# Retention scores in 64x64 quadrants, ordered ahead of the state product, with k transposed unscaled

## The chip, the cores and the metric

The kernel runs on one core of one Trainium2 chip. The metric is device time in microseconds (us) of one execution, as the median of several runs. Engines are named as in the profile: PE (TensorE's matmuls), PEld (its weight loads), DVE (VectorE), ACT (ScalarE), POOL (GpSimd) and SP (SyncE, which issues most transfers).

## What is computed

Retention attention (scores with a decay of gamma to the distance, no softmax), then a mixture of experts with a noisy gate that picks two of eight, then a second dense layer pair. The change is in the attention alone:

```python
def _attn_ref(q, k, v):                      # (4, 8, 576, 64)
    scale = 1.0 / np.sqrt(D_)
    scores = scale * np.matmul(q, k.transpose(0, 1, 3, 2))
    gamma = 1.0 - 2.0 ** (-5.0 - np.arange(H, dtype=np.float32))
    rel = pos[:, None] - pos[None, :]
    Dmat = np.where(rel >= 0, gamma[:, None, None] ** rel[None, :, :], 0.0)
    return np.matmul(scores * Dmat, v)

def reference(**kwargs):
    attn_out = _attn_ref(**attn_kwargs)
    x = attn_out.transpose(0, 2, 1, 3).reshape(B * S, H * D)     # 2304 x 512
    x = _moe_ref(x=x, **moe_kwargs)          # gate, two experts of eight, w1, relu, w2
    return _moe2_ref(x=x, **moe2_kwargs)     # x @ w_in, gated, @ w_out
```

## The kernel before

The 2304 tokens are 18 tiles `t` of 128. A sequence has 576 tokens, four and a half tiles, so a pattern of nine tiles repeats (`m = t % 9`): tiles with m = 0 begin a sequence and have no state yet, tiles with m = 4 hold the end of one sequence and the start of the next, and tiles with m = 8 add nothing to the state. The eight heads lie in pairs: `a` is the pair, and a head of a pair takes 64 of the 128 rows.

A tile takes these steps. `load` brings k, q and v on SP's queue, three tiles ahead. `ks` and `qs` scale k and q by powers of gamma on DVE. `tr` transposes k (four 128x128 transposes on PE) and ACT evicts the result as `kT`. q arrives in a layout that needs no transposition. `qk` computes the scores of 128 keys by 128 queries for each head into two PSUM banks (`sc0`, `sc1`; tags `ga` and `gb`, one buffer each), and DVE multiplies each bank by a mask of zeros and ones into `pt`. `av` multiplies the state of the tiles before (`sbd`, 64x64 for each head) by q into `px` (two banks, of which one has the tag `tp` with a single buffer). `av2` adds masked scores times v to `px`, and ACT evicts `px` with a scale into `xT`. `kv` adds k transposed times v to the state in PSUM (`pS`), which ACT evicts to `sbd` for the next tile. `xt` transposes the output back to rows of tokens, which ACT evicts to `xrow`. For every three tiles `gsum` and `logit` compute the gate's logits.

The gate's routing is a generator, `route`, one for each group of three tiles. Its parts are divided by `yield`, and `rstep` runs the next part, so the places of `rstep` in the loop fix where the route's instructions stand on each engine. On DVE the parts are: copying the logits, four operations on `rw`, four that end in `nl`, MAX to `rd`, and the one-hot part `ixf`, `rm`, `ra`. The rank matmuls (L374 to L377) multiply `ra` by a triangle and by ones on PE, and a last DVE part turns the ranks into slots. `send` scatters a token tile's rows to the experts' regions in DRAM from POOL. `wstep` splits expert weights into two parts for the next stage, on ACT and DVE, in the later tiles.

The order of work is written out by hand in the loop of `attention`; each engine works through its instructions in that order. In an iteration `t` it is: `xt` of t - 1, `tr` of t + 2, `av`, `av2`, `kv`, scaling for t + 3, `qk` and the masks of t + 1, `gsum` on every third. Five `rstep` lie between. Ahead of the loop `busy` runs matmuls on zeros (`BZ`: 7, then 2), and `table` makes a table of decays for q from a small transfer `grow`.

## Time and profile before

| what | us |
|---|---|
| median of 3 runs | 947.82 |
| lowest and highest run | 944.35, 948.03 |
| profiled execution, its own time | 936.64 |
| its span in the trace | 934.5 |
| PE busy | 921.8 (99%) |
| DVE busy | 606.8 (65%) |
| ACT busy | 466.5 (50%) |
| POOL busy | 235.9 (25%) |

The attention ends where the experts' first matmul (L737) begins, at 95.07 us of the span; the rest of the span belongs to the two layers behind it. In a timeline, the first number is the start in us from the span's start, the second the time until the last of the row's instructions ended, and a bracket at the end tells how long the engine was idle ahead and what released it. Matmuls overlap, so the length of a step on PE is best read from its start to the start of the next.

### The profile page before, as it was taken

Reading aid. Unit: us, or ns where it says so; the run is one execution under the profiler, and the core shown is the slowest. Engines: PE = TensorE matmul, PEld = TensorE weight load, DVE = VectorE, ACT = ScalarE, POOL = GpSimd, SP = SyncE. Lnnn points to the kernel's source line nnn. Section 1 sums busy time; section 2 is a strip of 40 time slices with the busy share of each in tenths; the row PEclk is TensorE's granted clock in tenths of the full one; section 3 lists DMA queues with packets and bytes.
Section 4 is the critical chain, followed back from the end, with each engine's and each line's share of the span. In section 5 each row is a group of like instructions: output and inputs, shape, how many; then the busy total and the mean of one; then the engine's idle time right before and its main releaser. Section 6 shows DMA issues by size and latency. Waiting matters only on the chain.

```text
span 934.5 us, 17789 instructions
## 1 busy us (share of the span) xinstructions
PE 921.8 (99%) x6314; PEld 818.2 (88%) x6314; DVE 606.8 (65%) x1327; ACT 466.5 (50%) x1025; POOL 235.9 (25%) x324
## 2 busy tenths in 40 slices
PE   9999999999999999999999999999999999999996
PEld 6887888988988889888888899999889998999985
DVE  5787747878879797787847446545745554564442
ACT  4666435455564645545544445544554464455432
POOL 1345531324233242432400221042004113300000
PEclk9999999999999999999999999999999999999999
DMA  9964877859879688896636787877578676846541
GB/s 339 386 243 147 304 243 232 238 187 280 259 241 282 227 256 271 248 267 218 224 111 214 265 298 252 307 247 240 188 262 270 205 258 227 271 166 228 167 150 49
DMA packets 123742, 221.22 MB, mean 237 GB/s; under 512 B 13037, under 2 KB 60915, under 8 KB 123643
## 3 DMA queue, kind: packets, MB, share of 16 engines
q1 hardware_dynamic: 113819, 190.47, 61.9%
q0 software_dynamic: 9392, 28.73, 9.1%
q8 instruction: 52, 0.85, 0.4%
q10 hardware_dynamic: 432, 0.79, 0.2%
q14 instruction: 47, 0.39, 0.1%
HBM read 163.97 MB, written 55.97 MB: 235 GB/s over the span
## 4 chain that ended last, share of the span: by engine, by line
PE 86%; DVE 7%; DMA 3%; issue 1%; ACT 1%; POOL 1%; SPq 0%; DVEq 0%; ACTq 0%; POOLq 0%
PE p L754 39%; PE ga L737 12%; PE gb L737 9%; PE mga L1168 7%; PE p L1168 5%; PE mgb L1168 2%; PE mtp L1168 2%; PE sc L225 2%; DVE b L591 1%; PE px L249 1%; PE p L293 1%; DVE cvt L635 1%; PE p L209 1%; DMA xe<-s,free 1%; DVE h L796 1%
## 5 line engine op out<-in xcount | busy, mean ns | idle before, releaser
L754 PE MATMUL p<-b,h 128*120 128x512 f32 (+1 forms) x1056 | 260.9, 395 | 0.0
L754 PEld LDWEIGHTS p<-b,h 128*120 128x120 f32 (+1 forms) x1056 | 189.2, 185 | 41.4 <-DVE h L796 0.4
L754 PE MATMUL p<-b,b 128*128 128x512 f32 x768 | 180.0, 390 | 0.0
L754 PEld LDWEIGHTS p<-b,b 128*128 128x128 f32 x768 | 142.3, 188 | 28.2
L737 PE MATMUL ga<-x,b 128*128 128x360 f32 (+1 forms) x768 | 134.4, 324 | 2.9 <-DVE h L796 2.9
L737 PEld LDWEIGHTS ga<-x,b 128*128 128x128 f32 x768 | 124.6, 188 | 12.1 <-DVE h L796 7.7
L640 POOL TENSOR_TENSOR cvl<-cvl,cvs 128x256 f32<-128x256 f32 x64 | 50.3, 785 | 229.9 <-ACT cva L621 163.0
L591 DVE TENSOR_TENSOR b<-b,b 128x512 fp32r<-128x512 f32 x128 | 89.6, 734 | 13.2 <-ACT b L590 12.9
L737 PE MATMUL gb<-b,b 128*128 128x256 f32 x672 | 89.7, 283 | 0.0
L737 PEld LDWEIGHTS gb<-b,b 128*128 128x128 f32 x672 | 86.9, 190 | 1.2
L885 POOL DMA_INDIRECT s<-yd,slotc x36 | 36.4, 1011 | 166.9 <-DVE x L991 48.4
L590 ACT ACTIVATE b<-b 128x512 fp32r<-128x512 f32 x128 | 74.1, 626 | 0.0
L1206 DVE SCALAR_TENSOR_TENSOR b<-s,b 128x512 fp32r<-128x512 f32 x64 | 44.3, 693 | 44.9 <-ACT b L1205 42.0
L1205 ACT ACTIVATE b<-s 128x512 fp32r<-128x512 f32 x64 | 40.5, 632 | 59.3 <-DVE s L1203 56.8
L796 DVE SCALAR_TENSOR_TENSOR h<-gb,h 128x256 fp32r<-128x256 f32 (+1 forms) x64 | 27.7, 433 | 50.2 <-PE p L754 35.2
L641 POOL TENSOR_TENSOR cvl<-cvt,cvl 128x256 f32<-128x256 f32 x64 | 58.2, 909 | 5.0
L1202 ACT ACTIVATE s<-s,three 128x512 f32<-128x512 f32 x64 | 45.9, 717 | 24.8 <-DVE s L1189 23.2
L1168 PE MATMUL mga<-b,b 128*128 128x256 f32 x384 | 56.3, 283 | 0.0
L1189 DVE TENSOR_TENSOR s<-p,mc 128x256 f32<-128x256 f32 x32 | 13.6, 424 | 65.4 <-PE p L1168 60.1
L1168 PEld LDWEIGHTS mga<-b,b 128*128 128x128 f32 x384 | 52.6, 191 | 2.5
L1203 DVE SCALAR_TENSOR_TENSOR s<-s,s 128x512 f32<-128x512 f32 x64 | 44.0, 687 | 7.5 <-DMA paced<-s 4.9
L1173 ACT ACTIVATE mc<-mga 128x256 f32<-128x256 f32 x64 | 24.6, 384 | 48.2 <-PE mga L1168 48.0
(206 smaller groups left out, 1433.6 us busy)
## 6 DMA issues: line engine op xcount, KB each, us to landing
b<-wc SPq DMA_DIRECT2D x112, 512.0 KB
b<-in_moe_w_dram SPq DMA_DIRECT2D x64, 512.0 KB
wc<-b SPq DMA_DIRECT2D x32, 512.0 KB
s<-xe SPq DMA_DIRECT2D x140, 64.0 KB
s<-in_moe_w_in_dram SPq DMA_DIRECT2D x32, 256.0 KB
s<-in_moe_w_out_dram SPq DMA_DIRECT2D x32, 256.0 KB
b<-wc SPq DMA_DIRECT2D x32, 256.0 KB
yd<-s SPq DMA_DIRECT2D x24, 240.0 KB
```

What stands on the lines that cost most here:

```text
L590: self.nc.scalar.activation(h, a, AF.Copy)
L591: rest = lambda h=h, l=l, a=a: self.nc.vector.tensor_sub(l, a, h.bitcast(F32))
L640: nc.gpsimd.tensor_mul(lf, lf, s.bitcast(F32))
L641: nc.gpsimd.tensor_add(lf, t.bitcast(F32), lf)
L737: nc.tensor.matmul(p, a[k], b[:, k, :n], start=(i == 0), stop=(i == 11))
L754: nc.tensor.matmul(a[:R], x[:, c], y[:, fi, :], start=(first and i == 0), stop=(last and i == 2))
L796: nc.vector.scalar_tensor_tensor(hl, p, 0.0, hh.bitcast(F32), op0=OP.max, op1=OP.subtract)
L1168: nc.tensor.matmul(t, w[:, u, k], x[:, z, k], start=(first and i == 0), stop=(last and i == 5), skip_group_check=True)
L1202: nc.scalar.activation(r, x, AF.Relu, bias=self.three)
L1203: v.scalar_tensor_tensor(x, r, 6.0, x, op0=OP.min, op1=OP.mult)
L1205: nc.scalar.activation(h[:, 0], x, AF.Copy, scale=1.0 / 6.0)
L1206: v.scalar_tensor_tensor(h[:, 1], x, 1.0 / 6.0, h[:, 0].bitcast(F32), op0=OP.mult, op1=OP.subtract)
```

## The change

The scores of a tile are computed as 16 matmuls with 64x64 weights in place of 8 with 64x128: each takes half of the keys, so a head and a half of the keys lie in one quadrant of the array, as the heads of the state product do. The state product of the same tile follows directly, and the transposes come behind it.

k is transposed unscaled into `kT`, a buffer of its own (half of `vk`, where the scaled k was); `ks` scales k in place afterwards, for the state alone. The decay of k goes into a table `dm` (mask times decay, made once on DVE by `decays`), with which the scores are multiplied; for m = 4 a memset clears the part between the two sequences. The scale of q's side moves from the eviction of the output to that of the state, which becomes four ACT instructions of 64 columns in place of one of 256; the output's becomes two of 256 columns in place of four of 128 (eight of 64 for m = 4). The eviction behind `xt` is issued in the next iteration (`rows()`).

The loop's order becomes: `kv`, `av2`, eviction of the output, that of the transposes of t - 1, `qk` and `av` of t + 1, masks of t + 1, `qs` of t + 2, `gsum`, `tr` of t + 2, `xt` of t, and `ks` of t + 2; four `rstep` in place of five, and one `yield` less ahead of the rank matmuls except in the last group. At the start, `grow` moves to ACT's queue ahead of the table load, the loads come in another order, the warm-up matmuls go from 7 to 5, and k's scaling no longer stands ahead of its transposes.

```diff
-BZ = (7, 2)
+BZ = (5, 2)
...
+        nc.sync.dma_start(self.c[:, 0:C_IO], i["cst"][:, 0:C_IO])
+        self.grow = self.big([P, 2048], BF)[0:6, 0:640]
+        nc.scalar.dma_start(self.grow.bitcast(F32), i["cst"][0:6, C_W:C_W + 320])
         nc.scalar.preload_act_table_set("natural_log_exp_and_others")
...
+    def decays(self, s):
+
+        if s == 0:
+            self.dm = self.big([P, 2, 4, P])
+        gk = self.c[:, C_GK:C_GK + 8].rearrange("p (a s) -> p s a", s=2)
+        self.nc.vector.tensor_mul(self.dm[:, s], self.c[:, C_MK:C_MK + P][:, None, :].to_broadcast([P, 4, P]),
+                                  gk[:, s, :, None].to_broadcast([P, 4, P]))
...
-        self.nc.vector.tensor_mul(r["ks"], r["k"], gk[:, :, None].to_broadcast([P, H, D]))
+        self.nc.vector.tensor_mul(r["k"], r["k"], gk[:, :, None].to_broadcast([P, H, D]))
...
-            for s, p in enumerate((p0, p1)):
-                h = slice(s * 64, s * 64 + 64)
-                nc.tensor.matmul(p[:, a, :], r["kT"][h, a, :], r["qT"][h, a, :], start=True, stop=True)
-        for s, p in enumerate((p0, p1)):
-            nc.vector.tensor_mul(pt[:, s], p, mask[:, None, :].to_broadcast([P, 4, P]))
+            for j in range(2):
+                for s, p in enumerate((p0, p1)):
+                    h, k = slice(s * 64, s * 64 + 64), slice(j * 64, j * 64 + 64)
+                    nc.tensor.matmul(p[k, a, :], r["kT"][h, a, k], r["qT"][h, a, :],
+                                     start=True, stop=True)
+        return pt, (p0, p1)
+
+    def masks(self, t, pt, ps):
+        nc = self.nc
+        for s, p in enumerate(ps):
+            nc.vector.tensor_mul(pt[:, s], p, self.dm[:, s])
+        if t % 9 == 4:
+            nc.vector.memset(pt[0:64, :, :, 64:P], 0.0)
...
+    def px_out(self, t):
+        nc = self.nc
+        r, px = self.raw[t], self.px
+        for j in range(2):
+            if j and t + 1 == NT:
+                nc.vector.tensor_copy(r["xT"][:, j::2], px[j])
+            else:
                 nc.scalar.activation(r["xT"][:, j::2], px[j], AF.Copy)
...
-        nc.scalar.activation(self.sbd[(t + 1) % 2], self.pS, AF.Copy)
+        w = C_GQ + (t + 1) % 9 * 4
+        for a in range(4):
+            nc.scalar.activation(self.sbd[(t + 1) % 2][:, a], self.pS[:, a], AF.Copy, scale=self.c[:, w + a:w + a + 1])
...
         yield
         yield
-        yield
-        if g0 + 2 * G >= NT:
+        if g0 + G == NT:
+            yield
             yield
...
         self.busy(BZ[0])
         self.table()
-        self.ks(0)
         self.tr(0)
+        self.decays(0)
         self.qs(0)
-        self.ks(1)
-        self.qs(1)
+        self.decays(1)
         self.busy(BZ[1])
-        self.qk(0)
+        sc = self.qk(0)
         self.gate_w()
         self.tr(1)
-        self.ks(2)
-        self.qs(2)
-        self.late_consts()
+        self.ks(0)
+        self.masks(0, *sc)
+        self.qs(1)
+        self.ks(1)
...
+            self.kv(t)
+            if t == 0:
+                self.tr(2)
+            self.av2(t)
+            self.px_out(t)
+            if t:
+                rows()
+            self.rstep()
+            if t + 1 < NT:
+                sc = self.qk(t + 1)
+                self.av(t + 1)
+                self.masks(t + 1, *sc)
+                self.rstep()
+                if t + 2 < NT:
+                    self.qs(t + 2)
+                self.rstep()
+                if t % 3 == 2:
+                    self.gsum(t // 3)
+                if 0 < t < NT - 2:
+                    self.tr(t + 2)
+                rows = self.xt(t)
...
+                if t % 3 == 2:
+                    self.gate(t, groups)
+                self.rstep()
+                if t + 2 < NT:
+                    self.ks(t + 2)
...
             if t == GA:
                 while self.sent < EARLY:
-                    self.rstep()
+                    if not self.sq:
+                        self.rstep()
                     self.send()
```

How that stands on the engines, at three places. PE in a steady tile before, from the last scores of tile 7 on (`sc` and `p` are PSUM tiles, `b` tiles in SBUF, `s_80` the state, `px` the output): scores, transposes of the output (L293) and of k (L209), state product (L239), values (L249).

```order
L225 MATMUL sc_689<-b_435 128x128
L225 MATMUL sc_690<-b_435 128x128
L293 MATMUL p_713<-cst,x_664 128x128 x4
L209 MATMUL p_722<-cst,b_617 128x128 x4
L239 MATMUL px<-b_435,s_80 64x128 x2
L239 MATMUL p_741<-b_435,s_80 64x128 x2
L239 MATMUL px<-b_435,s_80 64x128 x2
L239 MATMUL p_741<-b_435,s_80 64x128 x2
L249 MATMUL px<-b_688,b_436 64x128 x2
L249 MATMUL p_741<-b_688,b_436 64x128 x2
L249 MATMUL px<-b_688,b_436 64x128 x2
L249 MATMUL p_741<-b_688,b_436 64x128 x2
```

The same place after: the last scores of tile 7 (L229), state product (L250), transposes of k (L215) and of the output (L301), state update (L287), values (L260).

```order
L229 MATMUL sc_734<-b_503,b_504 64x128
L229 MATMUL sc_735<-b_503,b_504 64x128
L250 MATMUL px<-b_503,s_80 64x128 x2
L250 MATMUL p_753<-b_503,s_80 64x128 x2
L250 MATMUL px<-b_503,s_80 64x128 x2
L250 MATMUL p_753<-b_503,s_80 64x128 x2
L215 MATMUL p_773<-cst,b_604 128x128 x4
L301 MATMUL p_781<-cst,x_722 128x128 x4
L287 MATMUL p_161<-b_504,b_503 64x64 x8
L260 MATMUL px<-b_733,b_504 64x128 x2
L260 MATMUL p_753<-b_733,b_504 64x128 x2
```

The state product moved up to the scores, and the state update came ahead of the values.

PE at the rank matmuls of the group of tiles 3 to 5 before, behind the scores of tile 8:

```order
L225 MATMUL sc_780<-b_525 128x128
L225 MATMUL sc_781<-b_525 128x128
L374 LDWEIGHTS ones
L374 MATMUL p_220<-macc,ones 128x8
L377 LDWEIGHTS tri
L377 MATMUL p_220<-ra,tri 128x8
```

And after, from the end of the state product of tile 8 on:

```order
L250 MATMUL px<-b_604,s_79 64x128 x2
L250 MATMUL p_855<-b_604,s_79 64x128 x2
L215 MATMUL p_873<-cst,b_697 128x128 x4
L301 MATMUL p_879<-cst,x_722 128x128 x4
L387 LDWEIGHTS ones
L387 MATMUL p_223<-macc,ones 128x8
L390 LDWEIGHTS tri
L390 MATMUL p_223<-ra,tri 128x8
```

The rank matmuls went behind the state product and both sets of transposes.

DVE ahead of the rank matmuls' operand `ra` of the same group before; L195 and L200 scale k and q, L227 are the masks of tile 8:

```order
L349 MAX mx<-nl 128x8 x3
L351 MAX_INDEX ix<-mx,nl 128x8 x3
L353 TENSOR_TENSOR rd<-mx 128x3
L358 CAST ixf<-ix 128x6
L360 TENSOR_TENSOR rm<-cst,ixf 128x48
L365 TENSOR_TENSOR ra<-rm 128x24
L195 TENSOR_TENSOR b_704<-b_703,cst 128x512
L200 TENSOR_TENSOR b_703<-b_703,s_112 128x512
L227 TENSOR_TENSOR b_779<-sc_780,cst 128x512
L227 TENSOR_TENSOR b_779<-sc_781,cst 128x512
```

And after; L201 scales k, L206 q, L236 are the masks of tile 8:

```order
L201 TENSOR_TENSOR b_604<-b_604,cst 128x512
L362 MAX mx<-nl 128x8 x3
L364 MAX_INDEX ix<-mx,nl 128x8 x3
L366 TENSOR_TENSOR rd<-mx 128x3
L236 TENSOR_TENSOR b_835<-sc_836,b_118 128x512
L236 TENSOR_TENSOR b_835<-sc_837,b_118 128x512
L371 CAST ixf<-ix 128x6
L373 TENSOR_TENSOR rm<-cst,ixf 128x48
L378 TENSOR_TENSOR ra<-rm 128x24
L206 TENSOR_TENSOR b_697<-b_697,s_110 128x512
L392 TENSOR_TENSOR macc<-macc,ra 128x8 x3
L201 TENSOR_TENSOR b_697<-b_697,cst 128x512
```

The masks of tile 8 came ahead of the part that makes `ra` (L371 to L378).

## Rows read from the trace of the kernel before

**Rows 1.** The page: busy time of each engine; PE's granted clock in 40 slices, in tenths.

```profile
PE 921.8 (99%) x6314; PEld 818.2 (88%) x6314; DVE 606.8 (65%) x1327; ACT 466.5 (50%) x1025; POOL 235.9 (25%) x324
...
PEclk9999999999999999999999999999999999999999
```

**Rows 2.** Timeline of PE, one steady tile (start, time, engine, line, operation, out<-in, shapes).

```profile
40.95 1.16 PE L225 MATMUL sc<-b 64*128 64x128 f32 x16
42.04 0.66 PE L293 MATMUL p<-cst,x 128*128 128x128 f32 x4
42.53 0.60 PE L209 MATMUL p<-cst,b 128*128 128x128 f32 x4
43.06 0.33 PE L239 MATMUL px<-b,s 64*64 64x128 f32 x2
...
43.22 0.28 PE L239 MATMUL px<-b,s 64*64 64x128 f32 x2
...
43.33 0.28 PE L239 MATMUL px<-b,s 64*64 64x128 f32 x2
...
43.66 0.44 PE L249 MATMUL px<-b,b 128*64 128x128 f32 x4
...
44.58 0.63 PE L281 MATMUL p<-b 128*64 128x64 f32 x16
45.15 0.49 PE L225 MATMUL sc<-b 64*128 64x128 f32 x4
```

**Rows 3.** Timeline of PEld in the state product of the same tile.

```profile
43.11 0.14 PEld L239 LDWEIGHTS px<-b,s 64*64 64x64 f32 x2
```

**Rows 4.** Timeline of DVE around the same tile.

```profile
39.72 0.18 DVE L331 TENSOR_SCALAR rw<-ru 128x24 f32<-128x24 f32 x1 [0.54 <-ACT ru L328]
...
40.46 0.68 DVE L195 TENSOR_TENSOR b<-b,cst 128x512 f32<-128x512 f32 x1
41.06 0.68 DVE L200 TENSOR_TENSOR b<-b,s 128x512 f32<-128x512 f32 x1
42.14 1.29 DVE L227 TENSOR_TENSOR b<-sc,cst 128x512 f32<-128x512 f32 x2 [0.39 <-PE sc L225]
43.34 0.17 DVE L340 TENSOR_TENSOR rln<-rln,ru 128x24 f32<-128x24 f32 x1
...
44.20 0.31 DVE L349 MAX8 mx<-nl 128x8 f32<-128x8 f32 x3
...
45.41 0.17 DVE L365 TENSOR_TENSOR ra<-rm 128x24 bf16<-128x24 bf16 x1
```

**Rows 5.** Timeline of all engines, start of the program.

```profile
4.04 0.69 DVE L195 TENSOR_TENSOR b<-b,cst 128x512 f32<-128x512 f32 x1 [2.62 <-DMA b<-in_k_dram]
...
5.37 1.11 PE L209 MATMUL p<-cst,b 128*128 128x128 f32 x4
...
6.52 0.60 ACT L211 ACTIVATE b<-p 128x512 f32<-128x512 f32 x1 [0.45 <-PE p L209]
...
7.26 1.97 PE L225 MATMUL sc<-b 64*128 64x128 f32 x16
...
12.68 1.16 PE L225 MATMUL sc<-b 64*128 64x128 f32 x16
```

**Rows 6.** Timeline of PE, values and state update of tile 13.

```profile
70.90 0.70 PE L249 MATMUL px<-b,b 128*64 128x128 f32 x3
...
72.29 0.68 PE L281 MATMUL p<-b 64*64 64x64 f32 x16
```

**Rows 7.** Timeline of PE, values of tile 17 and the experts' first matmul.

```profile
89.88 0.43 PE L249 MATMUL px<-b,b 128*64 128x128 f32 x2 [0.46 <-DVE b L227]
...
95.07 0.74 PE L737 MATMUL ga<-x,b 128*128 128x360 f32 x3
```

**Rows 8.** Timeline of ACT, two evictions of 64 columns.

```profile
31.01 0.31 ACT L268 ACTIVATE x<-px,cst 128x64 f32<-128x64 f32 x1
31.21 0.31 ACT L266 ACTIVATE x<-p,cst 128x64 f32<-128x64 f32 x1
```

More of the change, by code (lines that the diff above doesn't have):

```diff
@@ L35 @@
 BIG = 3.0e38
-C_ID, C_GK, C_GQ, C_MK, C_MM, C_IO, C_EB = 0, 128, 200, 272, 400, 528, 536
-C_EC, C_FO, C_PI = 544, 552, 568
-C_W = 569
+C_ID, C_GK, C_GQ, C_MK, C_IO, C_EB = 0, 128, 200, 236, 364, 372
+C_EC, C_FO, C_PI = 380, 388, 404
+C_W = 405
 def shape_consts():
@@ L182, in load @@
         vk = self.big([P, 2, H, D])
-        self.raw[t] = dict(k=kq[:, 0], q=kq[:, 1], v=vk[:, 0], ks=vk[:, 1])
+        self.raw[t] = dict(k=kq[:, 0], q=kq[:, 1], v=vk[:, 0], kT=vk[:, 1].rearrange("p (a s) d -> p a (s d)", s=2))
         self.load_of(t, names)
@@ L216, in qk @@
         r = self.raw[t]
-        mk = C_MM if t % 9 == 4 else C_MK
-        mask = self.c[:, mk:mk + P]
         pt = self.big([P, 2, 4, P])
@@ L222, in qk @@
         for a in range(4):
-            for s, p in enumerate((p0, p1)):
-                h = slice(s * 64, s * 64 + 64)
-                nc.tensor.matmul(p[:, a, :], r["kT"][h, a, :], r["qT"][h, a, :], start=True, stop=True)
-        for s, p in enumerate((p0, p1)):
-            nc.vector.tensor_mul(pt[:, s], p, mask[:, None, :].to_broadcast([P, 4, P]))
-        r["pt"] = pt
+            for j in range(2):
[10 more added lines that the diff above has]
+            nc.vector.memset(pt[0:64, :, :, 64:P], 0.0)
+        self.raw[t]["pt"] = pt
     def av(self, t):
@@ L254, in av2 @@
         r["xT"] = self.xg[g][:, :, t % 3 * P:t % 3 * P + P]
-        w = self.c[:, C_GQ + m * 4:C_GQ + m * 4 + 4]
-        if m == 0:
-            for j in range(2):
-                nc.scalar.activation(r["xT"][:, j::2], px[j], AF.Copy)
-        elif t + 1 == NT:
-            for j in range(2):
-                nc.vector.tensor_mul(r["xT"][:, j::2], px[j],
-                                     w[:, j::2, None].to_broadcast([P, 2, P]))
-        else:
-            n = 64 if m == 4 else P
-            for a in range(4):
-                nc.scalar.activation(r["xT"][:, a, :n], px[a % 2][:, a // 2, :n], AF.Copy, scale=w[:, a:a + 1])
-                if m == 4:
-                    nc.scalar.activation(r["xT"][:, a, n:], px[a % 2][:, a // 2, n:], AF.Copy, scale=self.c[:, C_GQ + 36 + a:C_GQ + 37 + a])
+    def px_out(self, t):
[5 more added lines that the diff above has]
+            else:
+                nc.scalar.activation(r["xT"][:, j::2], px[j], AF.Copy)
         self.send(r["xT"][:, 0])
@@ L293, in xt, with out @@
             nc.tensor.transpose(p[:, a, :], r["xT"][:, a, :], self.ident)
-        self.xrow[t] = self.row([P, DM])
-        nc.scalar.activation(self.xrow[t].rearrange("p (a d) -> p a d", a=4), p, AF.Copy)
-        self.send(self.xrow[t])
+        x = self.row([P, DM])
+        def out():
+            nc.scalar.activation(x.rearrange("p (a d) -> p a d", a=4), p, AF.Copy)
+            self.xrow[t] = x
+            self.send(x)
+        return out
     def gsum(self, g):
@@ L444, in attention @@
         self.load(0, "kq")
-        self.load(1, "kq")
-        self.nc.sync.dma_start(self.c[:, C_MK:], self.i["cst"][:, C_MK:C_W])
+        self.load(1, "k")
         self.load(0, "v")
-        self.load(2, "kq")
+        self.load(1, "q")
+        self.load(2, "k")
         self.load(1, "v")
+        self.load(2, "q")
         self.load(3, "kq")
+        self.nc.sync.dma_start(self.c[:, C_IO:], self.i["cst"][:, C_IO:C_W])
         self.load(2, "v")
@@ L474, in attention @@
                 self.w_load()
-            self.rstep()
-            if t:
-                self.xt(t - 1)
-                self.zero(t - 1)
-            if 0 < t < NT - 2:
-                self.tr(t + 2)
-            if t and t % 3 == 0:
-                self.gate(t - 1, groups)
-            self.rstep()
-            self.av(t)
-            self.rstep()
-            self.wstep(WM)
-            self.av2(t)
+            if t == 0:
+                self.av(t)
             self.kv(t)
@@ L492, in attention @@
                 self.tr(2)
-            if t + 1 == NT:
+            self.av2(t)
[16 more added lines that the diff above has]
+                rows = self.xt(t)
+                if t == 0:
+                    self.late_consts()
+                self.zero(t)
+                if t % 3 == 2:
[3 more added lines that the diff above has]
+                    self.ks(t + 2)
+            else:
                 xs = self.x_new(0)
```

27 lines of the change are left out of this document (5 added, 22 removed).

## The prediction, made before the changed kernel was run

> **What bounds the kernel now.** I read the busy shares first [rows 1]: TensorE (PE) is busy 921.8 of 934.5 us, with a granted clock of nine tenths or more in every slice, while VectorE (DVE) and ScalarE (ACT) have room (65% and 50%). So a change is worth what it takes out of PE's row of work, less any wait that it puts there. This one is confined to the attention stage, about the first 95 us, so I went on to PE's timeline of one steady tile [rows 2]. No idle time is marked; each step is worth the distance from its first start to the next step's: scores 1.09 (40.95 to 42.04), transposes of the output 0.49 and of k 0.53, state product 0.60 (43.06 to 43.66), values 0.92, state update 0.57; together 4.20 us. The stage is 18 such tiles, and its limit is this sum.
>
> **Part 1, scores in quadrants beside the state product.** The state product is the model, since it has the same tile (64x64 weights, 128 columns). Its 8 matmuls are 16 records, two passes each, and go four at once: the groups start at 43.06, 43.22, 43.33 [rows 2], which is 0.16 for the first and 0.11 for the next. From the third to the values (43.66) there is 0.33, two groups and 0.11 for leaving the form. So four groups at 0.11, 0.05 to enter and 0.11 to leave. The new scores are 16 matmuls of that form, 32 passes, 8 groups; with the 4 groups of the state product behind them and one entry and exit for both, 12 x 0.11 + 0.16 = 1.48 against 1.09 + 0.60 = 1.69: 0.21 a tile, 16 tiles have both steps, and the two first tiles (0 and 9) save 0.05 each. Sum -3.5. The trace has no scores in quadrants. If they went at the old pace of a pair of passes (1.09 / 8 = 0.137 a group), 8 x 0.137 + 0.44 + 0.16 = 1.70: no gain. I take 0.11, the row of the same shape, and keep 0 as the upper end; below -3.5 there is no reason to go, since nothing else leaves PE.
>
> That four go at once shows in one more row: the second group's weights load at 43.11 [rows 3], while the matmuls that began at 43.06 in the same quadrants are in flight until 43.39, and the group starts 0.11 to 0.16 behind the first for all of them. The Trainium skill ("TensorE: Matmul & The Clock Gate", Part 3, The mechanism) says that a weight load overlaps with matmuls in flight only where their row groups differ. By that, quadrants that share rows would take turns and the new scores would cost about double; the row speaks against it for the state product.
>
> **Part 2, what waits for DVE.** The old order has the rank matmuls (L374 to L377) of a routing group behind the scores; the new one has them behind two transposes, right ahead of state update and values, and their operand ra (one-hot sums) is made on DVE behind both masks of the *next* tile. From the end of the scores of tile 7, DVE has to do, in its new order: masks 1.20 (42.14 to 43.34), the four operations to log(1+exp) 0.74 (39.72 to 40.46), q's scaling 0.60, the rln to nl chain 0.86 (43.34 to 44.20), k's scaling 0.60 (40.46 to 41.06), masks of tile 8 1.20, and the two parts on either side of them, MAX to ra, 1.38 (44.20 to 45.41 + 0.17) [rows 4]. That is 6.58, with some 0.09 for the two hand-overs 6.67. PE needs for the same way one period, 4.20 - 0.21 = 3.99, and then the state product 0.44 with its exit 0.11 and two sets of transposes 0.53 + 0.49; since a matmul lasts 0.28 and the next one starts after 0.11, DVE is let go 0.17 later than PE: 3.99 + 1.57 - 0.17 = 5.39. The rank matmuls wait 1.28. Behind them in PE's queue stand the state update, the values and the next scores, so all of it is lost. This holds for the groups of tiles 3 to 5 and 6 to 8. For those of tiles 0 to 2 and 9 to 11, the first of the two tiles is 4 or 13, whose masks get a memset of 64 partitions x 512 elements. No such operation is in these rows; it lies between nothing and one mask of 512 elements, 0.60 [rows 4], and I take +0.5, nearer the mask, since the length is the same: 1.8 each. The last two groups have other distances (extra parts at tile 14, two added yields) and no wait by this sum. Sum 2 x 1.28 + 2 x 1.8 = +6.2. Bounds: DVE free at the scores of the next tile leaves masks 1.20 + ixf to ra 0.63 + 0.09 + 0.17 against 1.57, 0.5 each and, since the memset is then over, 2.1 in all; with DVE another 0.65 behind at each (one L201 more ahead), 8.8. I take the sum, since the order lists every operation in it.
>
> **Part 3, the start.** Now: k0 has landed by 4.04 (DVE's first scaling begins), its transposes start at 5.37 and last 1.11, their eviction at 6.52 takes 0.60, the first scores begin at 7.26, the scores of tile 1 at 12.68 [rows 5]. The path to the first scores is scaling k 0.69, the table's matmul, transposes, eviction. The raw transposition needs no scaling, the table's small transfer leaves on ACT's queue ahead of the table load, and two warm matmuls less stand ahead. The first scores then need k0, 1.1 of transposes and 0.6 of eviction: 4.3 + 1.7 = 6.0, and q's scaling behind the eviction of the table ends near 6.1; I put them at 6.15, -1.1. What follows could save as much again (state update and transposes of tile 2 stand ahead of the values now, under the masks), but k is scaled in front of the masks, loads come in another order, and PE goes at half pace here (the four transposes 1.11 against 0.60 in rows 2, the first scores 1.97 against 1.16); fewer warm matmuls may draw that out. I count a quarter: -1.35 at the scores of tile 1, with bounds -2.2 and 0.
>
> **Part 4, stalls that go, and the tail.** In tile 13 the values last 1.39 (70.90 to 72.29) [rows 6] against 0.92 in rows 2; 0.11 of the difference is leaving a form, since the state update there has half the rows, and 0.35 late masks, which the values follow by three steps only. The new order has the state update between as well: -0.35, upper end 0. At the last tile the values begin 0.46 late behind the masks (89.88) [rows 7]. In the new order two weight splits, two scalings and the route's chain stand ahead of those masks, and half of the output's eviction stands on DVE behind more of the route: from 0 to +1.5; I take +0.5, about the wait that is there now, once more.
>
> **Parts that cost nothing.** The two decay tables (2 x 0.69) lie under the first transposes. ACT's work stays about the same: four evictions of the state with 64 columns, 0.20 apart [rows 8], replace one of 256, and two of the output with 256 columns replace four of 128. The deferred eviction of the output's transposes is needed only by the scatters. SP and POOL pass the same transfers; MoE's first operands are tokens of the first four groups, sent near tile 14 as before.
>
> **Sum.** -3.5 + 6.2 - 1.35 - 0.35 + 0.5 = +1.5. The profiled execution took 936.64 us (span 934.5), so 938.1 by that; the median of the runs is 947.82, 11.2 above it, in work that the change leaves alone, so 949.3.
>
> **Rivals.**
> *No wait for ra* (PE loses its time elsewhere, or DVE is ahead): without the +6.2, -4.7: 943.1. For it: DVE is busy 65% only. Against: the order of its queue is fixed. With the low bounds of ranks and start (2.1, -2.2) it is -3.45, 944.4, which I count to "same".
> *State chain on ACT, slower.* In the new order the four state evictions (4 x 0.20), the output's first one and the bank that it frees stand between the values and the next state product, which follows only 0.88 of scores behind. ACT has four evictions, 0.80, an estimated 0.3 for the first output (one and a half of them) and hand-overs of 0.2 to do in 0.92 + 0.88: some 0.5 to spare. A wait shows once a kT eviction or split (0.5 to 0.6) runs ahead of it in ACT's queue; at 0.3 in 16 tiles +4.8: 954.1. Against: ACT is idle half the time.
> *Late DVE everywhere, slower.* Rank waits at 8.8 and no gain at the start: -3.5 + 8.8 - 0.35 + 0.5 = +5.5, 953.3.
> *Quadrants in two lots.* If the two key halves took turns, 16 x 0.11 + 0.44 + 0.16 = 2.36 a tile, +0.67 x 16 and +0.83 x 2, +12.4 in place of -3.5; the slack of 0.88 a tile takes 3.5 off the rank waits: +13.9, near 962. The Trainium skill's sentence above would give this one; rows 3 speak against.
>
> **How the numbers follow.** A run of this kernel can tell some 0.5% (4.7 us) from no change. Chances: forecast 0.45 (946 to 952.5); low bounds 0.15 (944 to 946), both "same"; no rank wait 0.20 (942 to 943.1), faster; ACT chain 0.08, late DVE 0.07, two lots 0.05, slower. Faster 0.20, same 0.60, slower 0.20. The range goes from 942.5 to 956: it holds everything but the two lots and the outer halves of the first and last cases.
>
> **What would show it.** In the profile after: scores and state product of a steady tile together 1.48; idle time ahead of L387/L390 released by ra, about 1.3 twice and 1.8 twice; first scores at 6.15, tile 1's at 11.3; values of tile 13 near 1.0; MoE's first matmul near 96.6 instead of 95.07 [rows 7]. The forecast is wrong if the rank matmuls wait for nothing, if the scores' groups are not 0.11 apart, or if a wait on px or on the state's eviction stands ahead of L250 in every tile.

## The result: 0.7% slower, and the profile after

| what | before | after |
|---|---|---|
| median, us | 945.44 (6 runs, 944.35 to 948.03) | 952.62 (6 runs, 950.57 to 954.59) |
| ratio, 95% interval | | 1.0073 (1.0051 to 1.0095) |
| experts' first matmul, us of the span | 95.07 | 109.24 |
| from there to PE's last matmul | 832.3 | 836.3 |

The page of the kernel after, the same two rows as in [rows 1]:

```profile
PE 929.4 (98%) x6600; PEld 819.9 (86%) x6600; DVE 609.4 (64%) x1330; ACT 466.8 (49%) x1036; POOL 234.0 (25%) x323
...
PEclk9999899999999999999999999999999999999999
```

The granted clock now dips once in the 40 slices, in the fifth, which is 95 to 119 us. The parts of a steady tile are as forecast. PE's timeline of tile 7 after, the counterpart of [rows 2]:

```profile
40.24 1.10 PE L229 MATMUL sc<-b,b 64*64 64x128 f32 x32
...
41.33 0.28 PE L250 MATMUL p<-b,s 64*64 64x128 f32 x2
...
41.76 0.66 PE L215 MATMUL p<-cst,b 128*128 128x128 f32 x4
42.25 0.60 PE L301 MATMUL p<-cst,x 128*128 128x128 f32 x4
42.78 0.69 PE L287 MATMUL p<-b,b 128*64 128x64 f32 x16
43.30 0.39 PE L260 MATMUL px<-b,b 128*64 128x128 f32 x4
```

Scores and state product start 40.24 and the transposes 41.76, 1.52 with a wait of some 0.05; in tiles without a wait they take 0.92 + 0.55 = 1.47, against 1.69 before. Such a tile takes 4.0 in place of 4.2 (tile 7 itself 4.1). The loss is elsewhere, most of it in idle time of PE. Two places show it. First, the scores of tile 8 in PE's timeline of the kernel after:

```profile
44.34 0.80 PE L229 MATMUL sc<-b,b 64*64 64x128 f32 x10
45.42 0.47 PE L229 MATMUL sc<-b,b 64*64 64x128 f32 x4 [0.29 <-issue]
46.18 0.86 PE L229 MATMUL sc<-b,b 64*64 64x128 f32 x18 [0.29 <-issue]
47.47 0.33 PE L250 MATMUL px<-b,s 64*64 64x128 f32 x2 [0.43 <-ACT x L274]
```

The scores come in three pieces with idle time between that nothing in the profile ends ("issue"), and with 0.43 of waiting for the output's eviction it is 3.13 until the state product begins, in place of 0.92. Such a place is called a slow stretch below. Second, the table of windows around tile 16 (stretch; busy time of PE, PEld, DVE, ACT and POOL with the number of instructions; granted clock, DMA's share, GB/s):

```profile
84.00:88.50 4.50, 4.48 (x75) 3.33 (x67) 3.14 (x9) 2.78 (x8) 1.25 (x3) 1.00 0.01 3
92.00:94.00 2.00, 0.72 (x8) 0.34 (x5) 0.00 (x0) 0.00 (x0) 1.56 (x5) 1.00 0.48 182
96.50:98.50 2.00, 2.00 (x11) 1.58 (x10) 1.97 (x7) 0.90 (x4) 0.00 (x0) 0.50 0.33 98
```

PE, which had 75 matmuls in the 4.5 us ahead of it, does 8 in 2 us, DVE and ACT stand too, and the granted clock then falls from 1.00 to 0.50 (1.2 GHz) and stays there to about 102 us. Scores and state product of tile 16 take 8.0 in place of 1.47. While it lasts, POOL's scatters run one behind the other. This profiled execution took 954.59, the longest of the six, 2.0 above their median.

### The profile page after: what moved, and what is told of

It reads as the page before. It is cut to its first block, busy times and chain, and to the rows that moved or that the text cites. A ratio compares the mean times of both kernels' runs of the same rounds, so it can differ in the third digit from the quotient of the medians.

```text
span 952.7 us, 18358 instructions
## 1 busy us (share of the span) xinstructions
PE 929.4 (98%) x6600; PEld 819.9 (86%) x6600; DVE 609.4 (64%) x1330; ACT 466.8 (49%) x1036; POOL 234.0 (25%) x323
## 4 chain that ended last, share of the span: by engine, by line
PE 85%; DVE 6%; ACT 3%; issue 2%; DMA 2%; POOL 1%; another core or an unknown queue 1%; SPq 0%; DVEq 0%; ACTq 0%; POOLq 0%
PE p L772 39%; PE ga L755 12%; PE gb L755 9%; PE mga L1186 7%; PE p L1186 5%; PE mgb L1186 2%; PE mtp L1186 2%; PE sc L229 2%; PE p L215 1%; PE p L287 1%; DMA s<-xe 1%; PE px L260 1%; DVE b L609 1%; DVE b L236 1%; DMA xe<-s,free 1%
## 5 line engine op out<-in xcount | busy, mean ns | idle before, releaser
L814 DVE SCALAR_TENSOR_TENSOR h<-gb,h 128x256 fp32r<-128x256 f32 (+1 forms) x64 | 27.7, 433 | 47.3 <-PE p L772 35.2
L814 DVE SCALAR_TENSOR_TENSOR h<-ga,h 128x360 fp32r<-128x360 f32 (+1 forms) x64 | 32.6, 510 | 23.4 <-ACT h L813 20.5
```

The costliest lines, as they stand in the source:

```text
L814: nc.vector.scalar_tensor_tensor(hl, p, 0.0, hh.bitcast(F32), op0=OP.max, op1=OP.subtract)
```

## Experiments

All times stand beside runs of the kernel before on the same chip. There were several chips: the kernel before takes 944 to 948 us (medians) on three of them and 935 on the one of the last two experiments, which is a finding of its own, below. The record does not say which chip the result and the first trace are from.

**A second trace of the kernel before.** No edit.

> The kernel before, unchanged, for a second trace: its profiled execution took 936.6 us, its six timed ones 944 to 948. Theory one (the shown profile is a short execution, and the others lose time behind the attention): the experts' first matmul again at 95 us of the span, total 944 to 948. Theory two (the attention itself varies): the first expert matmul at 99 to 105 us.

It took 944.87. The experts begin at 104.00, not 95.07, and from there to the end it takes 832.3 again: the difference lies in the attention, and the rest is the same. Windows of this second trace around tile 16 (columns as above):

```profile
86.00:88.00 2.00, 2.00 (x39) 1.66 (x38) 1.72 (x7) 1.57 (x4) 1.77 (x3) 1.00 0.60 234
88.00:90.00 2.00, 1.06 (x14) 0.65 (x13) 0.19 (x2) 0.00 (x0) 1.56 (x5) 1.00 0.37 139
90.00:92.00 2.00, 1.07 (x10) 0.97 (x10) 0.00 (x0) 0.30 (x2) 0.89 (x2) 0.88 0.67 256
92.00:94.00 2.00, 2.00 (x16) 1.78 (x15) 0.69 (x2) 1.97 (x9) 0.00 (x0) 0.50 0.05 15
```

And the same work in the trace from which the rows ahead of the prediction are:

```profile
84.00:86.00 2.00, 2.00 (x34) 1.47 (x34) 1.75 (x3) 1.77 (x5) 1.78 (x4) 1.00 0.68 264
```

In the second trace the same stretch as in the kernel after stands at tile 16: PE does 14 and 10 matmuls in 2 us, then the clock falls. In the first, the scatters run (POOL busy 1.78 of 2 us) and PE loses nothing. So slow stretches come without the change too, and the trace on which the forecast rests had none of them. Scatters alone do not make one either: in the second trace POOL is as busy with them from 86 to 88 us, and PE does its 39 matmuls.

**The scores in the old form, in the new order.**

```diff
-            for j in range(2):
-                for s, p in enumerate((p0, p1)):
-                    h, k = slice(s * 64, s * 64 + 64), slice(j * 64, j * 64 + 64)
-                    nc.tensor.matmul(p[k, a, :], r["kT"][h, a, k], r["qT"][h, a, :],
-                                     start=True, stop=True)
+            for s, p in enumerate((p0, p1)):
+                h = slice(s * 64, s * 64 + 64)
+                nc.tensor.matmul(p[:, a, :], r["kT"][h, a, :], r["qT"][h, a, :], start=True, stop=True)
```

> The changed kernel with the scores in the old form, 8 matmuls with 64x128 weights; order and all else stay. In the changed kernel's trace the scores of tiles 8, 11 and 16 take 3.1, 3.2 and 8 us with the state product in place of 0.92 and 1.47, in pieces of some 8 instructions each 0.72 us, while scattered rows are being written. Theory A (the quadrants take their instructions so fast, 96 in 1.47 us, that the supply runs dry while scatters move): no such stretch, scores and state product 1.70 in every tile, attention ends at 97 to 100 us instead of 109, time 943 to 948. Rival B (order or waits make the stretches): they stay, time 952 to 956.

950.45, ratio 1.0063 (1.0046 to 1.0080). The stretches stay (tile 8 2.86, tile 11 2.89; from the scores of tile 16 to those of tile 17 10.7, where the kernel after has 12.7 and a tile without a stretch 4.0 to 4.2), and attention ends at 109.07. Theory A in its form of that time, that the quadrants' instruction rate makes the stretches, is wrong. The time, 950.45, lies below the range of rival B as well.

**The scores in quadrants, in the old order.** The same lines the other way round, in the kernel before.

> The kernel before with the scores alone in quadrants, order and all else as before. Theory A: scores 1.04 in place of 1.09 where no scatter moves, and stretches of 1 to 3 us more in a few tiles from tile 7 on; attention ends at 97 to 103 us, time 946 to 953. Rival B: no stretch, attention ends at 94 to 95 us, time 943 to 946.

950.89, ratio 1.0074 (1.0058 to 1.0091). Scores take 1.04 where nothing disturbs, as expected, but stretches stand at seven tiles (the scores take 2.0 to 2.2 at tiles 7, 8, 10 and 11, 1.8 at tile 13 and 3.0 at tile 14; at tile 15 it is the transposes and values) and attention ends at 107.9 instead of 104.0. So the form costs too where stretches occur; a reason may be that 32 instructions more per tile are 32 more to be supplied. This and the last run cannot be added up (1.0063 and 1.0074 against 1.0073 for both together), which was the reason to look at the stretches themselves.

**Scatters released by the state's eviction.** `send` is taken out behind `tr`, `px_out` and `xt` and stands twice behind the four evictions in `kv` (in tiles with m = 8, which have no `kv`, twice behind the output's eviction):

```diff
             nc.scalar.activation(self.sbd[(t + 1) % 2][:, a], self.pS[:, a], AF.Copy, scale=self.c[:, w + a:w + a + 1])
+        self.send(self.sbd[(t + 1) % 2][:, 3])
+        self.send(self.sbd[(t + 1) % 2][:, 3])
```

> The changed kernel with the scatters of the attention released by the eviction of the state, two behind one another, in place of by three other evictions: the rows of a scatter move some 1.4 us after its issue, so they would move beside transposes, state update and values, and not beside the scores. Theory A with the moving rows as the cause: tiles 8 and 11 fall to 1.5, the stretch at tile 16 stays in part since its scatters are issued in one row, time 946 to 951. Rival A2 (it is POOL's issuing, not the moving rows): the issue now falls on the scores, stretches in most tiles from 6 on, time over 955.

951.47, ratio 1.0077 (1.0059 to 1.0096), just above theory A's range and not told apart from the kernel after by time. In the trace the scores of tiles 8 and 11 take 1.09 in place of 3.1; the values of tiles 7 and 10, ahead of them, beside which the rows now move, take 0.7 more, and the run of six at tiles 15 and 16 costs as before. The stretch follows the scatters, but the sum of time stays (attention ends at 107.5 in this trace, 109.2 in that of the kernel after).

**All early scatters in one place, first try.** The 24 scatters of the first twelve tiles are issued behind the values of the last tile, in the kernel before and in the kernel after; `send` returns at once until then, and the rows to be scattered get other buffers so that they can wait.

```diff
+        if not self.sq or self.hold:
+            return
...
+                self.hold = False
+                while self.sent < EARLY:
+                    if not self.sq:
+                        self.rstep()
+                    self.send()
```

> The kernel before with no scatter during the attention: the 24 scatters of the first twelve tiles are issued in one row behind the values of the last tile (the scattered rows get other buffers so that they can wait), and the experts start some 35 us later, so the total says nothing and only the attention's steps are read. Theory A (PE's instructions come slowly while scattered rows move, whatever the form): no step of the attention over its usual time but for waits that the trace names, values of tile 17 begin at 88 to 91 us (99.1 in the second trace of the kernel before), granted clock 1.0 throughout. Rival B (the slow stretches have another cause, as the fetch of program blocks): they stay at places like tiles 7, 14, 16, values of tile 17 at 94 to 100.

> The changed kernel with the same: no scatter during the attention, 24 in one row behind the values of the last tile; only the attention's steps are read. Theory A: tiles 8, 11 and 16 at 1.47 for scores and state product, the rank matmuls wait at all four groups (1.2 at the two that waited before, 0.5 to 1.3 at the two whose wait the slow stretches had covered), values of tile 17 at 87 to 91 us (103.8 in the changed kernel's trace), so level with the kernel before without scatters or up to 2 us off. Rival B: slow stretches stay.

It did not do what it should. POOL had nothing else to wait for, ran ahead, and issued six scatters in a row as soon as a group's slots were known. That made it a dose instead: values of tile 17 began at 112.7 (before) and 116.6 (after), against 99.1 and 103.8 in their own traces, and every new stretch stands at a run of six. Rival B is not excluded by it.

**All early scatters in one place, held by the last tile's output.**

```diff
                 self.hold, r17 = False, self.raw[t]["xT"]
+                self.send(r17[:, 0])
```

> As the first run of this kind on the kernel before, with what it lacked: there POOL, which runs ahead of the other engines, issued each group's six scatters in one row as soon as their slots were known, and the slow stretches stood at these rows (tiles 7, 10, 13, 16). Here the first scatter is released by the output of the last tile, so none moves during the attention; the experts start some 35 us later and only the attention's steps are read. Theory A (PE's instructions come slowly while scattered rows move): no slow stretch, granted clock 1.0, values of tile 17 begin at 87 to 91 us (99.1 in the second trace of the kernel before, 112.7 with rows of six). Rival B (another cause): slow stretches stay, 94 or later.

> The same with the changed kernel. Theory A: scores and state product 1.47 in tiles 7, 10, 13 and 16, no slow stretch; rank matmuls wait 1.2 twice and 0.6 twice, as in the trace with rows of six (sum 3.6); values of tile 17 begin at 87 to 91 us (103.8 in the changed kernel's trace), within 2 us of the kernel before in the same form. Rival B: slow stretches stay, 96 or later.

Now nothing moves before 94 us. PE's waits from 20 to 92 us (total, times, longest), first the kernel before held, then the kernel after held:

```profile
PE px L249 <- DVE b L227: 0.6, 2, 0.5
```

```profile
PE p L399 <- DVE ra L387: 4.2, 4, 1.1
PE px L250 <- ACT x L274: 0.6, 1, 0.6
PE sc L229 <- ACT s L291: 0.6, 2, 0.3
PE px L260 <- DVE rw L353: 0.4, 2, 0.2
```

"Issue" is gone from both lists, which in the kernel after, from 20 to 110 us, held among others:

```profile
PE sc L229 <- issue: 1.8, 6, 0.3
PE p L250 <- issue: 1.7, 3, 1.0
...
PE px L250 <- issue: 1.1, 3, 0.5
```

Values of tile 17 begin at 89.5 in the kernel before held and at 90.5 in the kernel after held, against 99.1 and 103.8 with scatters. So without moving rows there is no stretch, in either kernel, and B, a cause that has nothing to do with the scatters, falls. Together with the two runs ahead, in which the stretches went with the scatters, this bears theory A out in a weaker form: while scattered rows move PE can stand with nothing in the profile that ends its wait, whatever the form, but it does not always. By these differences the kernel before loses 9.6 us and the kernel after 13.3. They set traces of different chips side by side: the held kernels ran on one where the kernel before takes 948 us, and from which the only trace with the scatters in the attention is that of five parts and paced scatters, below (0.7 us of "issue" waits ahead of 112 us).

**A fifth part of the routing in each iteration.**

```diff
+            self.rstep()
             self.kv(t)
...
         yield
         yield
-        if g0 + G == NT:
-            yield
-            yield
+        yield
+        yield
```

> The changed kernel with a fifth part of the routing in each iteration (ahead of the state update) and two yields more ahead of the rank matmuls, so that these stand in the same place with their operand made one part earlier, and the late groups are routed as early as in the kernel before. Theory C (the loss is in the routing's order: rank waits 2 x 1.2 and the late tokens' scatters 2.4 us later behind the attention, 2.6 us of waiting at 48 to 56 us of the experts): rank waits under 0.2, first scatter behind the attention at 1 to 2 us instead of 4.4, rest behind the attention 833 instead of 836; time 946 to 949. Rival D (the loss is in the number and rate of PE's instructions while scatters move): 950 to 953.

948.20, ratio 1.0009 (0.9993 to 1.0026): six of the seven us come back, as theory C said, with as many matmuls as in the kernel after. The profiled execution is a long one (951.57, 3.4 above the median); its attention ends at 107.2, and slow stretches are still there. The wait 50 us into the experts is down from 2.6 to 0.4; without the 2.7 of one wait that comes and goes (below) the rest takes 832.9. The rank waits are gone as well, but another came in their place, as PE's waits show:

```profile
PE px L250 <- ACT x L274: 3.6, 7, 1.0
PE sc L229 <- issue: 2.9, 7, 1.0
PE px L250 <- ACT s L291: 1.3, 1, 1.3
...
```

The seven waits come to 3.6. The fifth part puts the routing's exponential (L369) on ACT ahead of the state's evictions, where it waits for DVE's `rd`; the output's eviction and with it the bank for the next state product come late, as ACT's timeline of this kernel shows:

```profile
30.87 0.20 ACT L369 ACTIVATE e<-rd 128x3 f32<-128x3 f32 x1 [2.67 <-DVE rd L366]
30.98 0.91 ACT L291 ACTIVATE s<-p,cst 128x64 f32<-128x64 f32 x4
31.77 0.40 ACT L274 ACTIVATE x<-px 128x256 f32<-128x256 f32 x1
```

and PE's behind it:

```profile
32.22 0.33 PE L250 MATMUL px<-b,s 64*64 64x128 f32 x2 [0.97 <-ACT x L274]
```

**Five parts and paced scatters.** The edit of the scatters released by the state's eviction and that of the fifth part together, and the first loads of scattered rows two tiles later (`GA` 16), so that no six scatters stand in a row.

> The kernel with five parts in each iteration, and the scatters two for each tile, released by the eviction of its state; the run of six in one row at tile 14 is spread over tiles 14 to 16 and the first loads of scattered rows come two tiles later. Theory A: the long stretch at tile 16 (4.7 us and a halved clock behind it) falls to 1 to 2 us, attention ends at 100 to 104 us (107.2 with five parts alone), time 943 to 947. Rival B: no change against five parts alone, 947 to 949; rival E (the first loads become the bound): the experts' first matmul waits for the loads, 948 to 952.

951.98, ratio 1.0040 (1.0020 to 1.0061): rival E, by which the first loads of scattered rows become the bound. The scores of tile 16 take 0.93 again, but the experts' tokens come late, in PE's timeline:

```profile
105.58 1.03 PE L724 MATMUL p<-cst,s 120*128 120x120 f32 x4 [3.89 <-DMA s<-xe]
```

**Two routing parts more at the end only.**

```diff
+            if t > 14:
+                self.rstep()
             self.kv(t)
```

> The changed kernel with one part of the routing more in each of tiles 15 to 17 and nothing else: the late groups are routed as early as in the kernel before, the waits of the rank matmuls in tiles 4 and 13 stay. It splits what five parts everywhere won back. Theory C1 (the late tokens' scatters and loads): the wait of 2.6 us some 50 us into the experts goes, first scatter behind the attention 1 to 2.5 us after its end instead of 4.4, time 2 to 4 us under the changed kernel, 0.3 to 0.5% over the kernel before. Theory C2 (the rank waits and what follows from them): 0.6 to 0.8% over, as the changed kernel.

941.88 against 935.29 on this chip, ratio 1.0073 (1.0059 to 1.0087). It doesn't tell what it should: the rank matmuls of the group of tiles 12 to 14 now stand in tile 17 and wait 2.1 us themselves. But this trace has no stretch beside any of its scatters, so it shows the rank waits at all four tiles where they were forecast, and what comes behind them (PE's waits from 25 us on):

```profile
PE p L390 <- DVE ra L378: 6.7, 5, 2.1
...
PE p L724 <- DMA s<-xe: 1.7, 1, 1.7
```

The five are 1.08, 1.04, 1.02 and 1.43 at tiles 4, 7, 10 and 13, and the new one, 2.14; the last row is the experts' first transposes, which wait for the loads of scattered rows, a wait that no other trace with these loads in their usual place has. Ahead of the new rank wait this trace has reached 90.65, where the first trace of the kernel before begins the values of tile 17 at 89.88 [rows 7]: without stretches the steps are again within 1 us of each other. Behind the experts' start the late tokens cost 0.4 in place of 2.6, as in the kernel with five parts, which is theory C1's part of the loss; what C1 and C2 forecast for the time is not told apart, since the new waits of 2.1 and 1.7 stand in it.

**Five parts and the scores in the old form.** The second edit in the kernel with five parts.

> The kernel with five parts in each iteration, its scores in the old form of 8 matmuls with 64x128 weights: what the quadrants alone are worth in the new order. Theory A1 (the shorter scores count): 0.22 us in each of 18 tiles more, time 3 to 5 us (0.3 to 0.5%) over the kernel with five parts, so 0.4 to 0.6% over the kernel before. Theory A2 (twice the score instructions cost as much in the slow stretches beside scatters as the form saves): within 0.2% of the kernel with five parts, 0 to 0.3% over the kernel before.

938.96 against 935.29, ratio 1.0035 (1.0022 to 1.0048). Its trace has no stretch either. The first of its waits is the one that the fifth part made, `px` behind ACT:

```profile
PE px L248 <- ACT x L272: 4.0, 5, 1.2
```

The kernel with five parts in quadrants wasn't run on this chip, so A1 and A2 are not told apart; by the steps, an estimate, quadrants would take some 16 x 0.22 = 3.5 off these 938.96.

The kernel after itself wasn't run on this chip either, so what it loses where there are no stretches was not measured. None of these kernels beats the kernel before; one with the fifth part's exponential placed behind the state's evictions, which might take the 3.6 to 4.0 us of waits for `x` away, wasn't tried.

## Why the forecast came out as it did

The time lies in the range, but the likeliest case was "same" at +1.5 us and it became +7.2, slower. That it lies in the range is in part luck: the range was wide for other reasons than those that came. By the steps of the prediction:

| step | forecast | measured |
|---|---|---|
| scores and state product, a tile | 1.48 | 1.47 |
| rank waits, four groups | 1.28, 1.28, 1.8, 1.8 | 1.03, 1.02, 1.09, 1.08 (held) |
| memset in tiles 4 and 13 | in the rank wait | 0.18 + 0.28 each, ahead of it |
| first scores; scores of tile 1 | 6.15; 11.3 | 6.22; 11.84 |
| values of tile 13 | 1.0 | 1.37 |
| experts' first matmul | 96.6 | 109.24 |

**Part 1 was right**, to 0.01: quadrants of the scores go four at once, as the state product's do, 32 passes in 0.92. Where rows 3 and the Trainium skill's sentence ("TensorE: Matmul & The Clock Gate", Part 3, The mechanism) spoke against each other, the row decided, and the kernel after bears it out wherever no stretch falls on the scores; "two lots", 16 x 0.11 = 1.76 for these scores, is out.

**Part 2, the mechanism was right and its size 20% too high.** The rank matmuls wait for `ra`, which DVE makes behind the masks of the next tile. In PE's timeline after, at tile 4:

```profile
27.86 0.44 PE L260 MATMUL px<-b,b 128*64 128x128 f32 x4 [0.18 <-DVE rw L344]
...
29.24 1.10 PE L229 MATMUL sc<-b,b 64*64 64x128 f32 x32 [0.28 <-ACT s L291]
...
31.64 0.17 PE L387 MATMUL p<-macc,ones 128*128 128x8 bf16 x1
32.89 0.17 PE L390 MATMUL p<-ra,tri 128*128 128x8 bf16 x1 [1.08 <-DVE ra L378]
```

The sum of DVE's operations gave 1.28; without scatters it is 1.02 to 1.03. The memset took 0.48 on DVE,

```profile
27.33 0.48 DVE L238 MEMSET b<- 64x512 f32 x1 [0.17 <-DVE b L236]
```

but not as part of the rank wait: PE lost 0.18 ahead of the values and 0.28 ahead of the next scores, and came so much later to the rank matmuls. With the four rank waits (4.2) and twice 0.46 PE lost 5.1 where I had 6.2. In the kernel after itself only two of the four show, since in tiles 8 and 11 the slow stretch had let DVE catch up.

**Part 3 is not settled.** In this trace the first step comes out (6.22), and tile 1's scores gained 0.84 over [rows 5], not 1.35. But the start differs from trace to trace by as much: with the same code up to there, tile 1's scores begin at 11.51 to 12.90 in four traces with the start of the kernel before and at 10.54 to 12.51 in seven with the start of the kernel after.

**Part 4 is wrong in its first half.** The values of tile 13 gained 0.02 (1.37 against 1.39 in [rows 6]), since the memset made the next late. In the tail PE loses 0.65, about the size taken, but not by late masks. In the kernel after held, timeline of all engines, two weight splits on ACT (L618) stand ahead of the evictions of the state and the output, and the state product of tile 17 waits for the bank:

```profile
87.05 1.14 ACT L618 ACTIVATE b<-b 128x512 fp32r<-128x512 f32 x2
...
89.33 0.33 PE L250 MATMUL px<-b,s 64*64 64x128 f32 x2 [0.65 <-ACT x L274]
```

That is the rival of the state chain on ACT, in one tile.

So the sum of parts 1 to 4 came out near (without scatters the values of tile 17 begin 1.0 us later than before), by errors that cancel: 1.1 too much in part 2, some 0.8 too much gain in parts 3 and 4. **Two steps failed.** One stands under "Parts that cost nothing": that the scatters go out "near tile 14 as before". I looked at which transfers pass which queue, and not at when their slots are known. With four parts an iteration in place of five, the last early scatters and the loads behind them come later (first load 96.6 against 92.7 in the second trace of before), and the late tokens' first scatter comes 4.4 us behind the start of the experts instead of 1.5. This is the row of that scatter in POOL's timeline of the kernel after (experts' start 109.24), behind two rows of DVE:

```profile
112.02 0.53 DVE L814 SCALAR_TENSOR_TENSOR h<-ga,h 128x360 fp32r<-128x360 f32 x1 [2.10 <-ACT h L813]
...
113.15 0.17 DVE L401 CAST slots<-sf 128x6 int32<-128x6 f32 x1
...
113.60 1.25 POOL L427 DMA_INDIRECT xe<-s,slots  x1 [18.69 <-DMA b<-in_moe_w_dram]
```

The slots are ready at 113.32, since the last part of the routing stands on DVE behind the experts' first product (L814), which waited 2.10. (POOL's row names a transfer of weights as its releaser; that it played a part is not shown.) The same scatter in the second trace of before (experts' start 104.00), where the slots are ready ahead of that product:

```profile
105.49 0.97 POOL L414 DMA_INDIRECT xe<-s,slots  x1 [14.60 <-DVE slots L388]
```

Fifty us later the experts wait for these tokens, 0.85 and more in a chain of DVE and ACT behind their loads, in the timeline of the kernel after:

```profile
157.12 0.73 DVE L708 STREAM_TRANSPOSE xp<-s 128x512 f32<-128x512 f32 x1 [3.85 <-DMA s<-xe]
157.94 0.60 ACT L710 ACTIVATE x<-xp 128x512 fp32r<-128x512 f32 x1 [5.13 <-DVE xp L708]
...
158.87 1.28 PE L772 MATMUL p<-b,h 128*128 128x512 f32 x3 [0.85 <-ACT h L813]
```

By 56 us behind the experts' start the kernel after has lost 2.6 us on the second trace of before, 0.5 of it at 12 us and the rest from 44 us on; with five parts it is 0.4, and with two parts more at the end 0.4 too. The other step is the sentence that put the profiled 936.64 beside the median of 947.82 and called the 11.2 us between them "work that the change leaves alone". It was the attention: in a second trace that takes the usual time, 8.9 of it (104.00 against 95.07) are, nearly all, slow stretches in the very stage that the change rearranges. A profile that is 1.2% under the median of its own kernel was the sign that a term was missing, and I carried the difference over.

The account of the difference between the second trace of before and that of after, up to PE's last matmul (5.2 in the attention, 4.1 behind it, 9.3 us in all): +1.0 by the steps to the values of tile 17, +3.7 by longer slow stretches (13.3 against 9.6), +0.5 between the values and the experts, +2.6 by the late tokens, and 1.4 at one wait of PE for ACT near 580 us. It is more than the 7.2 between the medians, since the profiled execution of the kernel after was its longest. The last term comes and goes: the same wait is 2.7 in the kernel with five parts and in the kernel after held, and the other traces have none. It stays open.

Why the stretches are longer can be read further from the runs on record. Counted from the first scores of tile 1 to the first values of tile 17, which leaves the start out, in us:

| scores, order | with scatters | without | lost |
|---|---|---|---|
| old form, old order (second trace of before; held) | 86.2 | 78.0 | 8.3 |
| quadrants, old order | 91.5 | 77.1, estimate: 17 x 0.05 less | 14.4 |
| old form, new order | 92.2 | 82 to 84, estimate: 80.0 and 17 x 0.22, less what the waits for DVE shrink by | 8 to 10 |
| quadrants, new order (after; held) | 92.0 | 80.0 | 12.0 |

In both orders the loss is the larger with quadrants. So what the quadrants take off the steps, up to 3.7 us, the stretches took back in the main, and the order's waits and the late tokens remained; it fits that the old form in the new order is no slower than the kernel after (1.0063 and 1.0073). These are single traces, the held ones from another chip than the first three with scatters, and the kernel after held has waits (the ranks of tiles 7 and 10) that the stretches cover in the kernel after. How the form lengthens the stretches is not shown.

Of the rivals, "late DVE everywhere" was nearest in time (953.3) and wrong in its cause. The state chain on ACT came in the kernel after only at tiles 8, 11 and 12, in or right behind stretches (1.1 in all), but it is what the fifth part ran into, with 3.6 to 4.0 us in all.

## What to carry to other kernels

When a profiled execution lies further from the median than the runs from each other, find where before forecasting; take a second trace and compare stage by stage. A written-out order has a pace for side work: one part less in each iteration makes every chain that hangs on it later, down to transfers 50 us away, and it is to be counted like any moved instruction. A step moved ahead in a waiting engine's queue (the exponential ahead of the evictions) wins back one wait and makes another. A form with more instructions a tile can lose in stretches beside transfers what its steps save, so it is to be tried with and without those transfers.

## What the runs showed of the hardware

While rows of an indirect scatter move, PE can stand idle with nothing in the profile that ends it. Its work then comes in pieces some 0.7 us apart: at tile 16 of the kernel after they begin at 90.18, 90.91, 91.68, 93.10, 93.84, 94.56, 95.27 and 96.00, and the 16 passes of the state product take from 90.99 to 96.59, where they take 0.55 in a tile without a stretch. That it is the supply of instructions that fails is argued from this, not shown. DVE stands longer there than PE makes it: the scores of tile 16 end at 91.37, and its masks begin at 96.14, in DVE's timeline:

```profile
96.14 1.29 DVE L236 TENSOR_TENSOR b<-sc,b 128x512 f32<-128x512 f32 x2 [6.59 <-remote]
```

("remote" is a releaser that the profile cannot name.) In the second trace of before DVE and ACT only wait for PE. This is a scatter of the run at tile 16 in POOL's timeline of the second trace of before:

```profile
88.56 0.97 POOL L414 DMA_INDIRECT xe<-s,slots  x1 [0.22 <-issue]
```

and PE's state update beside it:

```profile
88.00 0.32 PE L281 MATMUL p<-b 128*64 128x64 f32 x3
88.72 0.34 PE L281 MATMUL p<-b 128*64 128x64 f32 x3 [0.40 <-issue]
89.43 0.39 PE L281 MATMUL p<-b 128*64 128x64 f32 x6 [0.36 <-issue]
```

On three chips the traces have such stretches, which by the held kernels put the values of tile 17 off by 9.6 us in the kernel before and by 13.3 in the kernel after, from some 90 us. On a fourth, where the kernel before takes 935 us, the two traces (two routing parts more, and five parts with the old scores) have none, with the scatters there all the same. The first trace of the kernel before (936.64) has none either and is like that chip in time; which chip it is from is not known. What supplies the instructions and why one chip is free of it, no run here shows: packets of the instruction queue (16 KB each) lie near some stretches and not near others. And behind the stretch at tile 16, in which PE was busy 0.72 to 1.07 of 2 us, the granted clock fell from 1.00 to 0.50 (from 2.4 to 1.2 GHz), for 3.4 us in the second trace of before and 6.8 us in the kernel after, where the transposes behind the stretch took 0.91 in place of 0.49.
